# Attention fused with two MLPs on one core: row loads of the norms held behind key loads, queries loaded to 64 partitions

## The chip, the cores and the metric

One core of a Trainium2 chip. The time is device microseconds from launch to end of the whole fused kernel, median of several runs; one further execution was profiled. Engines: TensorE (PE, with its weight loads PEld), VectorE (DVE), ScalarE (ACT), GpSimd (POOL) and SyncE (SP, which here only issues DMAs).

## The reference

Attention over 4 x 12 heads, 448 rows, head size 64, then two MLPs over all 1792 tokens:

```python
def rmsnorm(x, g):
    rms = np.sqrt(np.mean(x * x, axis=-1, keepdims=True) + 1e-06)
    return x / rms * g
q_n, k_n = (rmsnorm(q, g_q), rmsnorm(k, g_k))
scores = scale * np.matmul(q_n, k_n.transpose(0, 1, 3, 2))
attn = softmax(scores)
x = np.matmul(attn, v)              # to (1792, 768)
x = ((x @ w1) * (x @ w2)) @ w3 @ w_out
h = x @ w_in
out = (h * np.clip(h + 3.0, 0.0, 6.0) / 6.0) @ w_out2
```

## The kernel before, in words

A "unit" i is a pair of heads; there are 24. A "row" t is one step of the loop at the end of `attention`: unit t // 8, score tile t % 8. In each row the loop traces one score product (two matmuls, high and low part of the keys, L536 and L537), its scaling with the norms and row maximum on DVE (L543), an exponential on ACT (L555), the transposes and value product of a unit 8 rows back, then `fill`, and then the tasks that `at(t, ...)` has put on this row. `fill` adds the other work: the product W' = w3 w_out in the first third (`wprime`), later the first MLP (`layer1`, `layer2`), with the conversion of 64-bit weights (`convert`, L135 to L141, three DVE operations a piece). All loads go through one in-order SP queue (`dma`, L88).

The order written is only a priority: a scheduler simulates the program and places every instruction of an engine as early as its operands and its buffers allow; on the chip each engine then runs its list in order. `tc.issue_after(x)` adds one constraint: what is issued inside it stands behind x on x's engine.

The norms of a unit pair g need the rows of q and k with the 64 numbers of a row along the free axis. `load_nat` (L409) fetches them (tile nat, 112 x 1024, 448 KB, two buffers). `ssq` squares on ACT (L436), `ssum` reduces on DVE (L442), `rms1` (L448 to L451) and `rms2` (L460 to L466) take the inverse root for the pair, `small1` transposes it on PE (L477) and `small2` copies it, writes it to DRAM (rkd) and reads it back spread over partitions (rb), which the unit's first L543 needs. Task rows for an even unit i: square of unit i+2 at row 8i, reduction at 8i+2, `load_nat(i+4)` at 8i+3 and `load_nat(i+5)` at 8i+4, `rms1` at 8i+6, `rms2` at 8i+6, `small1` at 8i+8.

Keys and queries come a second time, head dimension on partitions: `load_k` (tile kr, one buffer, row 8i+5 for unit i+2) and `load_q` (tile qr, one buffer, row 8i+3 for unit i+2). Both DRAM arrays hold the 64 rows twice, one copy over the other. `qhi` writes Q = round(q g) on all 128 partitions (ACT, L505), `qlo` puts the rest q g - Q over partitions 64 to 127 (DVE, L510), so one product takes the high and the low part of the query. `ksplit` writes K in two parts (ACT L516, POOL L517).

`load_nat(i)` tries to hold itself behind the key load of unit i-2: `T.get(("kl", i - 2))`. A key load is known there only once `load_k` has been traced, and `load_k(i+2)` is traced at row 8i+5.

Of the kernel before, what the change touches and what calls it, by code (L numbers as in the profile page):

```python
# [12 lines left out]
F32 = mybir.dt.float32  # L13
# [3 lines left out]
AF = mybir.ActivationFunctionType  # L17
# [5 lines left out]
B, H, S, D = 4, 12, 448, 64  # L23
HP = H // 2
NP = B * HP
P = 128
# [20 lines left out]
def fused_kernel(ctx: ExitStack, tc: tile.TileContext, nat, qT, kT, vin, gq, gk,  # L47
                 w12, w3t, wo, win, wo2, outT):
    nc = tc.nc
# [15 lines left out]
    G = gs[:, 2:3]  # L65
# [21 lines left out]
    def dma(out, src):  # L87
        return nc.sync.dma_start(out, src)  # L88
# [7 lines left out]
    def at(t, fn, *a):  # L96
        tasks[max(t + SHIFT.get(getattr(fn, "__name__", ""), 0), now[0])].append((fn, a))
# [304 lines left out]
    T = {}  # L402
    anchors = {}

    def attention(ap, rate):
# [3 lines left out]
        def load_nat(i):  # L409
            if i < NP:  # L410
                T["nat", i] = ap.tile([CP, 4 * NC, D], F32, tag="nat", bufs=2, name="nat")
                a = T.get(("kl", i - 2))
                with ExitStack() as es:
                    if a is not None:
                        es.enter_context(tc.issue_after(a.ins))
                    dma(T["nat", i], nat[i].rearrange("p a b d -> p (a b) d"))

        def load_q(i):
            T["qr", i] = ap.tile([P, 2, S], F32, tag="qr", bufs=1, name="qr")
            dma(T["qr", i], qT[i])  # L420

        def load_k(i):
            T["kr", i] = ap.tile([P, 2, S], F32, tag="kr", bufs=1, name="kr")
# [78 lines left out]

        def qhi(i):
            T["Q", i] = q = ap.tile([P, 2, S], F32R, tag="Q", bufs=2, name="Q")
            nc.scalar.activation(q, T["qr", i], AF.Copy, scale=G)  # L505

        def qlo(i):
            a = slice(64, 128)
            q = T["Q", i]
            nc.vector.scalar_tensor_tensor(out=q[a], in0=T["qr", i][a], scalar=G[a, :], in1=q[a],  # L510
                                           op0=ALU.mult, op1=ALU.subtract)

        def ksplit(i):
# [133 lines left out]
        groups = {s: [s, s + 1] for s in range(0, NP, 2)}  # L647

        load_nat(0)
        load_nat(1)  # L650
        dma(gs[:, 0:1], gq)
        dma(gs[:, 1:2], gk)
        nc.vector.tensor_mul(G, gs[:, 0:1], gs[:, 1:2])
        load_q(0)
        load_k(0)
        open_wprime()
# [10 lines left out]
        first = ExitStack()  # L667
        first.enter_context(tc.issue_after(T["rbl"].ins))
        qhi(0)
        qlo(0)  # L670
        ksplit(0)
        for z in range(10):
            prep[0].step()
        load_q(1)
        load_k(1)
        for z in range(16):
            prep[0].step()
        load_nat(2)
        load_nat(3)

        for i in range(NP):
            t = 8 * i
            n = i + 1
            if n < NP:
                at(t, qhi, n)
                at(t + 1, qlo, n)
                at(t + 2, ksplit, n)
            at(t - 4, load_v, i)
            if i + 2 < NP:
                at(t + 3, load_q, i + 2)  # L690
                at(t + 5, load_k, i + 2)
            at(t + 1, vsplit, i)
            if i % 2 == 0 and i + 2 < NP:
                g = groups[i + 2]
                at(t, ssq, i + 2)
                at(t + 2, ssq, i + 3)
                at(t + 3, ssum, i + 2, g)
                at(t + 3, load_nat, i + 4)
                at(t + 4, ssum, i + 3, g)
                at(t + 4, load_nat, i + 5)  # L700
                at(t + 5, rms1, g)
                at(t + 6, rms2, g)
                at(t + 16, load_rb, i + 3)

            u = t + LG
            at(u + 2, rsum1, i)
            at(u + 6, xcopy, i, 0)
            at(u + 7, xadd, i, 0)
            at(u + 8, small1, i, None)
            at(u + 9, small2, i, None)  # L710
            at(u + 9, xcopy, i, 1)
            at(u + 10, xadd, i, 1)
            at(u + 13, xout, i)
            if i % 2 == 0 and i + 2 < NP:
                g = groups[i + 2]
                tasks[t + LG] = [z for z in tasks[t + LG] if z[0] is not small1]
                tasks[t + LG + 1] = [z for z in tasks[t + LG + 1] if z[0] is not small2]
                at(t + LG, small1, i - 1, g)
                at(t + LG + 1, small2, i - 1, g)

        t = -1
# [36 lines left out]
    with tc.tile_pool(name="att", bufs=2, side="left") as ap:  # L758
        attention(ap, rate)
# [45 lines left out]
    step, q = 0, 0  # L805
# [126 lines left out]
```

## Time and profile before

| | us |
|---|---|
| median of 3 runs | 1272.6 (1270.17 to 1278.13) |
| profiled execution, device time | 1276.18 |
| span of its profile, first to last instruction | 1274.3 |
| PE busy in the span | 1183.1 |
| DVE busy in the span | 795.1 |

A row of a stretch reads: its length, then for each engine the busy time and the number of instructions, the granted TensorE clock as a share of full speed (2.4 GHz), the mean busy share of the 16 DMA engines, and the GB/s that they moved. A row of a group of instructions reads: line, engine, operation, output and inputs, shapes, count, then busy us, mean ns of one, and the idle time of the engine just before them.

### The profile page before, as it was taken

The page shows a single profiled execution, that of the slowest core. Times are in us where ns is not written, and L with a number is a line of the kernel's source. Part 1 is how long each engine was busy: PE and PEld are TensorE (multiplying, and loading weights), DVE is VectorE, ACT ScalarE, POOL GpSimd, SP SyncE. Part 2 cuts the span into 40 slices and gives each one's busy share as a digit, 9 for nine tenths or more (in the row PEclk, how much of TensorE's full clock was granted, in tenths as well). Part 3 has the DMA queues.
Part 4 walks back from the last instruction along what each step waited for, and adds up shares of the span by engine and source line. Part 5 has one row for each costly group of instructions (what it writes and reads, how often), then busy time and mean ns, then how long its engine had stood idle before and what let it go on. Part 6 is the DMA issues. An engine that isn't in the chain of part 4 may idle for free.

```text
span 1274.3 us, 16884 instructions
## 1 busy us (share of the span) xinstructions
PE 1183.1 (93%) x5868; PEld 1033.9 (81%) x5868; DVE 795.1 (62%) x1524; ACT 678.8 (53%) x1305; POOL 463.6 (36%) x292
## 2 busy tenths in 40 slices
PE   3587998888889999999999999889999999999998
PEld 2355987667668999999998998778999999999997
DVE  6989789989993578768643446994433343343332
ACT  5887667866783566766642223444533353344332
POOL 4334324624443112222111003445454454545542
PEclk9698998989999999999999999899999999999999
DMA  7898664666688666676349983450100020001001
GB/s 248 253 256 243 202 193 167 194 229 228 211 274 306 209 217 199 235 225 220 134 163 382 348 323 113 158 173 25 60 28 1 1 87 1 1 1 44 1 1 44
DMA packets 64693, 203.72 MB, mean 160 GB/s; under 512 B 8544, under 2 KB 25440, under 8 KB 64608
## 3 DMA queue, kind: packets, MB, share of 16 engines
q1 hardware_dynamic: 64608, 202.65, 48.2%
q8 instruction: 46, 0.75, 0.2%
q14 instruction: 39, 0.32, 0.1%
HBM read 173.93 MB, written 28.68 MB: 159 GB/s over the span
## 4 chain that ended last, share of the span: by engine, by line
PE 67%; DMA 11%; DVE 10%; issue 5%; ACT 3%; POOL 2%; SPq 1%; DVEq 0%; POOLq 0%; ACTq 0%
PE bank L80 8%; PE bank L82 8%; PE bank L81 8%; PE acc L81 6%; PE acc L82 6%; PE acc L80 5%; PE h L80 5%; PE h L81 5%; PE h L82 5%; PE bank L562 3%; DMA raw<-in_w_dram 2%; DVE wf L141 2%; DMA wr<-in_wo_dram 2%; PE bank L536 2%; PE bank L537 2%
## 5 line engine op out<-in xcount | busy, mean ns | idle before, releaser
L800 POOL TENSOR_TENSOR wis<-wf,wis 128x768 fp32r<-128x768 f32 x63 | 119.8, 1902 | 234.1 <-ACT wis L799 234.1
L872 DVE SCALAR_TENSOR_TENSOR u<-u,h 128x448 f32<-128x448 f32 x64 | 39.5, 618 | 217.3 <-ACT u L871 217.3
L800 POOL TENSOR_TENSOR wos<-wf,wos 128x768 fp32r<-128x768 f32 x64 | 119.0, 1860 | 103.6 <-ACT wos L799 103.6
L80 PE MATMUL bank<-xhl,ws 128*128 128x448 f32 x384 | 145.1, 378 | 7.7 <-ACT ws L285 6.3
L543 DVE CUSTOM_DVE_ANT_0 PP<-bank,rb,rq 112x448 f32<-112x448 f32 x192 | 129.1, 677 | 31.9 <-PE bank L537 27.4
L82 PE MATMUL bank<-xhl,ws 128*128 128x448 f32 x384 | 143.9, 375 | 4.9 <-POOL ws L287 4.9
L81 PE MATMUL acc<-g,wos 128*128 128x448 f32 x384 | 144.3, 376 | 3.8 <-DVE g L876 3.7
L555 ACT ACTIVATE PP<-PP,mx 112x448 f32<-112x448 f32 x192 | 127.4, 664 | 37.4 <-DVE mx L550 34.2
L80 PE MATMUL acc<-g,wos 128*128 128x448 f32 x384 | 138.5, 371 | 5.5 <-ACT g L875 5.5
L82 PE MATMUL acc<-g,wos 128*128 128x448 f32 x384 | 143.2, 373 | 0.0
L81 PE MATMUL bank<-xhl,ws 128*128 128x448 f32 x384 | 142.5, 371 | 0.1
L80 PE MATMUL h<-x2h,wis 128*128 128x448 f32 x378 | 139.0, 368 | 0.0
L81 PE MATMUL h<-x2h,wis 128*128 128x448 f32 x378 | 138.9, 368 | 0.0
L82 PE MATMUL h<-x2h,wis 128*128 128x448 f32 x378 | 137.5, 364 | 0.4 <-POOL wis L800 0.4
L876 DVE TENSOR_TENSOR g<-u,g 128x448 fp32r<-128x448 f32 x64 | 97.9, 1529 | 33.6 <-ACT g L875 33.6
L871 ACT ACTIVATE u<-h,half 128x448 f32<-128x448 f32 x64 | 40.4, 631 | 143.2 <-PE h L82 143.2
L536 PE MATMUL bank<-K,Q 128*112 128x448 f32 x192 | 78.3, 409 | 37.5 <-DVE mx L543 25.0
L562 PE MATMUL bank<-ident,PP 112*128 112x112 f32 x672 | 97.0, 267 | 11.8 <-DVE xl L581 10.2
L562 PEld LDWEIGHTS bank<-ident,PP 112*128 112x128 f32 x672 | 80.5, 145 | 33.8 <-DVE xl L581 13.3
L571 ACT ACTIVATE xh<-bank 128x448 fp32r<-128x448 f32 (+1 forms) x156 | 83.0, 537 | 43.3 <-PE bank L562 38.4
L581 DVE TENSOR_TENSOR xl<-bank,xh 128x448 fp32r<-128x448 f32 x142 | 87.1, 615 | 25.5 <-ACT xh L571 23.8
L799 ACT ACTIVATE wos<-wf 128x768 fp32r<-128x768 f32 x64 | 54.1, 846 | 86.9 <-PE acc L82 86.7
(126 smaller groups left out, 2763.5 us busy)
## 6 DMA issues: line engine op xcount, KB each, us to landing
ws<-w12d SPq DMA_DIRECT2D x48, 768.0 KB, 5.1
ws<-wpd SPq DMA_DIRECT2D x32, 768.0 KB, 4.2
raw<-in_w_dram SPq DMA_DIRECT2D x32, 384.0 KB, 4.3
w12d<-ws SPq DMA_DIRECT2D x16, 768.0 KB, 6.0
wr<-in_win_dram SPq DMA_DIRECT2D x16, 768.0 KB, 4.5
wr<-in_wo_dram SPq DMA_DIRECT2D x16, 768.0 KB, 6.6
nat<-in_nat_dram SPq DMA_DIRECT2D x24, 448.0 KB, 5.9
qr<-in_qT_dram SPq DMA_DIRECT2D x24, 448.0 KB, 6.4
```

The lines of the kernel that those rows point to most:

```text
L80: nc.tensor.matmul(ps, lh, rh, start=first, stop=False)
L81: nc.tensor.matmul(ps, lh, rl, start=False, stop=False)
L82: return nc.tensor.matmul(ps, ll, rh, start=False, stop=last)
L536: nc.tensor.matmul(ps[:CP, :S], qs, k1[:, j, :], start=True, stop=False)
L543: anchors[8 * i + s].append(nc.vector.tensor_tensor_reduce(out=T["PP", i][:, c, sl], in0=ps[:CP, :S], in1=T["rb", i][:, sl], op0=ALU.mult, ...
L555: anchors[8 * i + s].append(nc.scalar.activation(v, v, AF.Exp, bias=T["m", i][:, 8 + s : 9 + s], accum_out=T["sum", i][:, s : s + 1]))
L562: nc.tensor.transpose(ps[:, c * CP : c * CP + CP], src[:, c, kb * P : kb * P + P], ident[:CP, :CP])
L571: nc.scalar.activation(hi, ps, AF.Copy)
L581: nc.vector.tensor_sub(lo, ps, hi)
L799: nc.scalar.activation(t[:, 0, :], wf[q], AF.Copy)
L800: nc.gpsimd.tensor_sub(t[:, 1, :], wf[q], t[:, 0, :])
L876: nc.vector.tensor_sub(g[:, 1, :], u, g[:, 0, :])
```

## The change

Three edits. `load_nat` moves three rows later, to 8i+6 and 8i+7, behind the row in which `load_k(i+2)` is traced, and falls back to the key load of unit i-3, so that both row loads of a pair stand behind `load_k(i+2)`. `load_q` fetches one copy of the queries to partitions 0 to 63 (224 KB in place of 448 KB). `qhi` writes the high part on 64 partitions, and `qlo` reads partitions 0 to 63 and writes 64 to 127.

```diff
         def load_nat(i):
             if i < NP:
                 T["nat", i] = ap.tile([CP, 4 * NC, D], F32, tag="nat", bufs=2, name="nat")
-                a = T.get(("kl", i - 2))
+                a = T.get(("kl", i - 2)) or T.get(("kl", i - 3))
...
         def load_q(i):
-            T["qr", i] = ap.tile([P, 2, S], F32, tag="qr", bufs=1, name="qr")
-            dma(T["qr", i], qT[i])
+            T["qr", i] = ap.tile([D, 2, S], F32, tag="qr", bufs=1, name="qr")
+            dma(T["qr", i], qT[i][:D])
...
-            nc.scalar.activation(q, T["qr", i], AF.Copy, scale=G)
+            nc.scalar.activation(q[:D], T["qr", i], AF.Copy, scale=G[:D, :])
 
         def qlo(i):
-            a = slice(64, 128)
             q = T["Q", i]
-            nc.vector.scalar_tensor_tensor(out=q[a], in0=T["qr", i][a], scalar=G[a, :], in1=q[a],
+            nc.vector.scalar_tensor_tensor(out=q[D:], in0=T["qr", i], scalar=G[:D, :], in1=q[:D],
                                            op0=ALU.mult, op1=ALU.subtract)
...
                 at(t + 3, ssum, i + 2, g)
-                at(t + 3, load_nat, i + 4)
+                at(t + 6, load_nat, i + 4)
                 at(t + 4, ssum, i + 3, g)
-                at(t + 4, load_nat, i + 5)
+                at(t + 7, load_nat, i + 5)
```

## Rows read from the trace of the kernel before

**Rows 1.** The page's first part: busy time of each engine over the span
```profile
PE 1183.1 (93%) x5868; PEld 1033.9 (81%) x5868; DVE 795.1 (62%) x1524; ACT 678.8 (53%) x1305; POOL 463.6 (36%) x292
```

**Rows 2.** Stretches of the attention: engines, clock, DMA share, GB/s
```profile
core 0: us, PE busy (x) PEld busy (x) DVE busy (x) ACT busy (x) POOL busy (x), PEclk, DMA share, GB/s
0.00:60.00 60.00, 26.25 (x78) 17.14 (x79) 49.19 (x108) 40.46 (x77) 23.32 (x20) 0.85 0.81 252
60.00:130.00 70.00, 56.65 (x243) 37.23 (x242) 64.93 (x152) 54.81 (x114) 27.44 (x21) 0.87 0.92 250
130.00:240.00 110.00, 101.85 (x550) 89.05 (x550) 94.03 (x238) 78.46 (x170) 38.54 (x27) 0.94 0.63 201
240.00:400.00 160.00, 138.76 (x687) 112.18 (x686) 141.85 (x338) 113.51 (x259) 76.25 (x57) 0.94 0.69 229
400.00:660.00 260.00, 260.00 (x1438) 235.81 (x1437) 169.39 (x412) 157.40 (x338) 54.82 (x39) 1.00 0.62 206
```

**Rows 3.** The chain of waits from 60 to 130 us, shares by line
```profile
by line: DMA raw<-in_w3t_dram 17.7%; DMA raw<-in_wo_dram 10.8%; DVE raw L136 7.8%; DMA rkd<-rks 7.6%; DMA rsd<-rss 6.6%; DMA rsb<-rsd 6.2%; DMA wpd<-wst 5.9%; DVE raw L138 5.5%; issue 5.5%; DVE raw L141 3.8%; DVE ss L442 3.6%; SPq L88 3.3%;
```

**Rows 4.** DMA issues by stretch: 0:60 (two), 60:130 (three), 130:240, 240:400
```profile
nat<-in_nat_dram SPq DMA_DIRECT2D x8, 448.0 KB, 9.3
kr<-in_kT_dram SPq DMA_DIRECT2D x5, 448.0 KB, 3.2
...
DMA packets 6593, 17.48 MB, mean 250 GB/s; under 512 B 865, under 2 KB 2273, under 8 KB 6586
nat<-in_nat_dram SPq DMA_DIRECT2D x12, 448.0 KB, 5.9
kr<-in_kT_dram SPq DMA_DIRECT2D x2, 448.0 KB
...
kr<-in_kT_dram SPq DMA_DIRECT2D x4, 448.0 KB, 3.3
...
kr<-in_kT_dram SPq DMA_DIRECT2D x6, 448.0 KB, 5.2
```

**Rows 5.** SP's queue in order of time: the key load of unit 6
```profile
121.68 0.33 SPq L88 DMA_DIRECT2D kr<-in_kT_dram  x1
```

**Rows 6.** DVE's groups from 60 to 130 us: the norms' reductions and arithmetic
```profile
L442 DVE TENSOR_REDUCE ss<-nat 112x16 f32<-112x1024 f32 x12 | 14.4, 1208 | 0.0
...
L461 DVE TENSOR_TENSOR rt<-rt,ss 112x32 f32<-112x32 f32 x5 | 1.8, 353 | 0.0
L462 DVE TENSOR_SCALAR rt<-rt 112x32 f32<-112x32 f32 x5 | 1.7, 348 | 0.0
L460 DVE TENSOR_TENSOR rt<-ry 112x32 f32<-112x32 f32 x5 | 1.7, 332 | 0.0
...
L464 DVE TENSOR_TENSOR rr<-ry,rt 112x32 f32<-112x32 f32 x3 | 1.1, 360 | 0.0
L448 DVE TENSOR_SCALAR ss<-ss 112x32 f32<-112x32 f32 x6 | 1.0, 169 | 0.0
```

**Rows 7.** DVE's groups from 240 to 400 us: the norms
```profile
L442 DVE TENSOR_REDUCE ss<-nat 112x16 f32<-112x1024 f32 x2 | 2.3, 1210 | 0.0
...
L460 DVE TENSOR_TENSOR rt<-ry 112x32 f32<-112x32 f32 x3 | 1.1, 373 | 0.0
```

**Rows 8.** The query's low part (min/median/max ns), then 128 partitions against 64
```profile
L510 DVE SCALAR_TENSOR_TENSOR Q<-qr,gs,Q x24: 1150/1635/3026, 10.1 to 595.6; 64x896 fp32r<-64x896 f32 x24
...
L581 DVE TENSOR_TENSOR xl<-bank,xh 128x448 fp32r<-128x448 f32 x58 | 35.7, 617 | 18.7 <-ACT xh L571 17.3
...
L583 DVE TENSOR_TENSOR xh<-bank,xh 64x448 fp32r<-64x448 f32 x10 | 6.2, 618 | 27.3 <-ACT xl L574 27.3
```

**Rows 9.** Stretches with loads to 128 partitions, then to 64 (columns as rows 2)
```profile
159.80:162.30 2.50, 2.50 (x17) 2.29 (x16) 2.47 (x10) 1.31 (x3) 0.00 (x0) 1.00 0.87 267
...
560.30:563.20 2.90, 2.90 (x18) 2.64 (x17) 2.09 (x5) 1.38 (x4) 0.00 (x0) 1.00 0.49 108
```

**Rows 10.** PE's waits from 0 to 60 us: who, total us, times, longest
```profile
PE bank L477 <- DVE rr L464: 2.3, 1, 2.3
```

## The prediction

> **What bounds the kernel now.** I read the page's first part, then stretches, then the chain, then the queues. Over the whole span PE is busy 93% [rows 1], but this is a mean over unlike stages. The stretches [rows 2] show two regimes: from 400 to 660 us PE has no idle time (260.00 of 260) and DVE has 91 us to spare; before 400 us PE is idle for 33.8, 13.4, 8.2 and 21.2 us, 76.5 in all, while DVE is busy 82% to 93%. So only what shortens the time up to 400 us counts, and what can be put off beyond it is free. The tightest stretch is 60 to 130 us: DVE 64.93 of 70, DMA share 0.92, both the highest of all, and a granted TensorE clock of 0.87, that is part of the time at 1.2 GHz, after the first stretch with its idle PE. The chain there [rows 3] is almost without PE: 28.5% are weight loads (raw), 26.3% the small transfers rkd, rsd, rsb and wpd, then the weights' conversion on DVE.
>
> In this stretch 12 of the 24 row loads of the norms are issued, after 8 before it, but only 7 key loads in both together [rows 4]. The row loads run up to ten units ahead of the units that need them. The code says why: at row 8i+3 the key load of unit i+2 isn't traced yet (row 8i+5), so the hold finds nothing and the scheduler places a row load as soon as a buffer is free. The DVE groups [rows 6] show the price: 14.4 us of reductions and 1.8 + 1.7 + 1.7 + 1.1 + 1.0 = 7.3 us of arithmetic, 21.7 of the 64.93.
>
> **The change, part by part.**
>
> *The hold.* Behind the change both row loads of a pair (i+4, i+5) stand behind the key load of unit i+2. From the counts of key loads [rows 4] I take what becomes due where. Up to 60 us five are issued (units 0 to 4), so pairs up to (6,7) are let go, as now; 60 to 130 us adds units 5 and 6, the latter only at 121.68 [rows 5], so pair (8,9) arrives at its end; 130 to 240 adds 7 to 10, 240 to 400 adds 11 to 16. One pair costs DVE two reductions of 1.21 us and about 7.3 / 5 = 1.5 us of arithmetic [rows 6], 3.9 us.
>
> From 60 to 130 us one pair, (6,7), is left of the norms: 21.7 - 3.9 = 17.8 us less DVE. The DMA loses ten row loads of 0.459 MB and two halves of a query load of 0.229 MB: 5.05 of 17.48 MB [rows 4]; at a share of 0.92 of 70 us for 17.48 MB, 3.7 us a MB, that is 18.6 us. Both limits thus give way by the same amount. PE comes next: it has 13.4 us of idle time in the stretch [rows 2]. I let the stretch shrink by these 13.4 us. The other ends: 17.8 if the clock also recovers (56.65 us x 0.87 = 49.3 at full clock, which fits into 52), and nothing if the waits for small transfers in the chain [rows 3] are a matter of their own latency.
>
> From 130 to 240 us two pairs are processed today and two after the change: no difference. From 240 to 400 us one pair's reductions (2.3 us) and three groups' arithmetic (3 x 1.5) are there today [rows 7], 6.8 us; after it three pairs, 11.7: 4.9 us more DVE. DVE is idle 18.2 us in this stretch [rows 2], so between 0 and 4.9 is paid; no row is nearer to one end, so I take the middle, 2.4. The six row loads that come into it, 2.75 MB, cost 160 x 0.69 / 36.6 (229 GB/s x 160 us) = 3.0 us a MB, 8 us of DMA time where 50 are idle, and six halved query loads take 1.4 MB back: nothing. Three pairs, (18,19) to (22,23), move beyond 400 us: 3 x 3.9 = 12 us DVE, hidden under its 91 idle there. The squares on ACT move with them and are covered, ACT being the less busy engine everywhere [rows 2].
>
> The SP queue: behind a key load that waits for its buffer now also stand two row loads. Behind these are weight loads; but today a row load waits for its own buffer in the same queue, so I count no difference, with the waits of PE named below as the risk.
>
> *The queries.* ACT and DVE still go through 896 columns. For DVE a 64-partition form takes as long as a 128-partition one, 618 against 617 ns, and the 64-partition row is one that writes partitions 64 to 127 from 0 to 63 as `qlo` will [rows 8]; `qlo`, 1150 ns at best and 1635 at the median, stays. I count 0 for ACT and DVE. The transfer is halved. Its price isn't in the trace, so by the nearest rows [rows 9]: with loads to 128 partitions the engines move 267 / 0.87 = 307 GB/s of busy time, in the stretch with the two 64-partition loads 108 / 0.49 = 220. A full query load is 0.459 / 307 = 1.49 us, a half one between 0.75 and 1.04 us. I take 1.04, a saving of 0.45 us. It tells only where the DMA presses and I have not counted it yet, from 0 to 60 us: five loads, 2.2 us, of which I put 1 us on the path (0 to 2.2).
>
> The Trainium skill (SBUF — State Buffer, section "Door 1: The DMA port swizzle") speaks against this part: 64 partitions from 0 reach only half of the ports, so half the bytes would go at half the rate. The rows lie between that rule and an unchanged rate (220 against 307, not 153). By the rule the 1 us would be 0 and the sum 11.0 in place of 12.0.
>
> *The sum.* -13.4 + 2.4 - 1.0 = -12.0 us. The profiled execution took 1276.2 us (a span of 1274.3 and 1.9 around it), which gives 1264.2; it lay 3.6 us above the median of the runs, so against that I predict 1272.6 - 12.0 = 1260.6 us. What is won before 400 us stays won, since afterwards PE goes through a fixed list without a gap.
>
> **Rivals.** About 1%, 12.7 us, is what a measurement of this kernel can tell from no change.
>
> *More than that.* Both resources keep their shares in the freed stretch, the clock recovers, the 4.9 us are covered: -17.8 - 2.2 = -20.0, 1252.6 us. For it: DVE and DMA give way alike. Against it: PE would need the full clock at once, and the chain holds latencies.
>
> *Hidden anyway.* The stretch is set by the latencies in its chain, rkd, rsd, rsb and wpd with 26.3%, and by weight loads whose place in the order stays [rows 3]. Then the relief is nothing, the late cost 2.4 and the queries -1: 1274 us. Against it: the raw loads, 28.5%, wait in a DMA queue of which 29% of the bytes go.
>
> *Slower: PE waits for the norms.* Today the scaled roots of a pair are ready long before the transpose (L477) that stands in PE's list two rows behind `rms2`; the one time this failed, in the first stretch, PE waited 2.3 us [rows 10]. With the rows held back, the chain load, square, reduction, root, transpose follows the key load by the length of DVE's and ACT's queues. It decides once the last multiply of a pair comes on DVE later than PE reaches its transpose. Eleven pairs at 2.3 us cost 25.3: 1260.6 + 25.3 = 1285.9. Against it: the load is let go at row 8i+5 and the transpose stands at row 8i+24, 19 rows later; from 60 to 130 us, the tightest stretch, two key loads and so two units of 8 rows are issued in 70 us, 4.4 us a row, so some 80 us of room.
>
> *The change doesn't do what it says.* If the hold changed nothing in the order, only the queries' 1 us would be left: 1271.6. As the key load of unit i+2 is traced one row ahead of the new place, I hold that for unlikely.
>
> **How the numbers follow.** The forecast, 7 to 17 us won: 0.45, about half of it on either side of 12.7. More: 0.20. Hidden: 0.20. Slower by waits: 0.12. No hold: 0.03. Faster by over 1%: 0.20 + 0.23 = 0.43; within: 0.22 + 0.20 + 0.03 = 0.45; slower: 0.12. The likeliest case's own range is 1255.6 to 1265.6. The range reaches from 1242, twice the sum's relief and more than the second case (the scheduler lays out the whole program anew), to 1282, short of the slower case.
>
> **What would show it.** Right: between two key loads two row loads, and the last pair's after the key load of unit 20 rather than by 230 us; in the stretch after 60 us fewer than four reductions, its DMA share clearly under 0.92; the last conversions of the first MLP's weights some 12 us earlier; `qlo` still at 1150 ns at best. Wrong: the units 2 to 4 at the same times as today in spite of fewer reductions (hidden), idle time of PE before L477 in many pairs (the slower case), or row loads as far ahead as today (no hold).

## The result and the profile after

The changed kernel takes 1288.6 us (median of 4, 1287.23 to 1291.69) against 1273.8 us of the kernel before beside it (median of 4, 1270.17 to 1278.13): a ratio of 1.0132, interval 1.0094 to 1.017. It is 1.3% slower, where 1260.6 us was forecast, and outside the range. The profiled execution took 1287.23 us with a span of 1285.5, 11.2 us more than the span before. (In the lines after, code below L506 stands one line higher than before: L542 for L543, L509 for L510, L561 for L562.)

The first view is the table of stretches, columns as in [rows 2]:

```profile
0.00:60.00 60.00, 27.68 (x69) 16.04 (x70) 46.62 (x102) 37.19 (x70) 22.96 (x20) 0.87 0.73 222
60.00:130.00 70.00, 66.26 (x327) 50.58 (x326) 58.17 (x144) 50.79 (x112) 30.05 (x22) 0.91 0.66 210
130.00:240.00 110.00, 93.73 (x498) 80.20 (x497) 97.72 (x240) 80.20 (x176) 42.10 (x29) 0.92 0.60 180
240.00:400.00 160.00, 133.64 (x626) 105.31 (x625) 139.87 (x329) 110.23 (x246) 69.23 (x51) 0.88 0.69 214
400.00:660.00 260.00, 258.17 (x1413) 232.72 (x1412) 171.19 (x427) 158.45 (x343) 51.42 (x37) 1.00 0.66 213
```

Read PE's count of matmuls, which is progress, against [rows 2]. From 60 to 130 us the forecast relief is there: 327 for 243, PE idle 3.7 us for 13.4, DMA share 0.66 for 0.92. From 130 to 240 us 52 matmuls are lost again (498 for 550), from 240 to 400 another 61 (626 for 687), 57 of them of the filler, which waits for the converted weights (274 for 331). In that last stretch PE is idle 26.4 us for 21.2, and its clock is granted at 0.88 for 0.94: one matmul takes 133.64 / 626 = 213 ns for 202. Over 626 matmuls that is 7.2 us, beside 5.1 us of idle time. The whole kernel shows the same: PE runs 5868 matmuls in both profiles, with 6.7 us more busy time after (1189.8 for 1183.1) and 4.5 us more idle time, so more than half of the loss is matmuls that took longer. DVE, of which the prediction feared more work from 240 to 400 us, is busy 139.87 us for 141.85: its total did not grow.

Where the order of loads changed shows in SP's queue in order of time, 270 to 372 us, row and weight loads of the first MLP (`raw<-in_w_dram`) alone:

```profile
274.71 1.29 SPq L88 DMA_DIRECT2D nat<-in_nat_dram  x2
279.37 3.46 SPq L88 DMA_DIRECT2D raw<-in_w_dram  x2
...
301.71 0.33 SPq L88 DMA_DIRECT2D raw<-in_w_dram  x1
...
333.79 0.89 SPq L88 DMA_DIRECT2D nat<-in_nat_dram  x2
336.66 0.35 SPq L88 DMA_DIRECT2D raw<-in_w_dram  x1
```

The hold does what it says: the row loads come in pairs behind every second key load, the first of each pair at 129, 176, 222, 275, 334, 388, 471 and 517 us; before, the last one was issued by 227 us. Three pairs thus come into the time in which the weights of the first MLP are loaded, converted and split, where there was none. The chain of waits from 280 to 372 us (start, us, what) says what that does; after:

```profile
by line: DMA raw<-in_w_dram 26.6%; issue 15.9%; POOL ws L287 6.9%; ACT PP L554 4.5%; DVE PP L542 4.0%; DVE raw L136 3.4%; PE bank L80 3.2%; PE bank L82 2.8%; PE bank L81 2.7%; ACT raw L135 2.6%; DVE raw L141 2.6%; PE bank L561 2.5%; ACT xh 
...
279.37 8.93 DMA raw<-in_w_dram
...
300.38 1.31 POOL ws L287
301.71 4.75 DMA raw<-in_w_dram
...
335.60 1.04 POOL ws L287
336.66 6.52 DMA raw<-in_w_dram
343.63 0.63 DVE raw L136
344.25 1.12 DVE ss L442
345.44 0.47 DVE raw L141
...
352.46 1.90 DVE ss L448
354.36 1.85 POOL ws L287
```

and before, the same stretch:

```profile
289.20 1.04 POOL ws L287
290.25 4.87 DMA raw<-in_w_dram
...
298.57 1.00 POOL ws L287
299.58 4.91 DMA raw<-in_w_dram
304.51 3.52 DMA raw<-in_w_dram
```

In both, most `raw` loads start just when a split on POOL (L287) ends: of the 25 that need a freed buffer, 22 before and 16 after start within 0.1 us of the end of the split that frees theirs. That is a loop of three buffers (L269): a piece is loaded, converted by ACT and DVE, split by ACT and POOL, and only then is its buffer free for the next load. What lengthens one turn of it delays the pieces behind. In these chains the piece of a load behind two row loads is 8.93 and 6.52 us long, that of the others 3.5 to 4.9. At 344.25 and 352.46 the norms' reduction and first root operation stand in the chain themselves, the latter with 1.90 us for what takes 0.17 at best (the last section says what held it). The share of the weight loads in the chain is no larger after (26.6% for 27.6%), and few of their landings were recorded: from 240 to 400 us five before, 3.4 to 6.2 us, and three after, 6.5, 6.6 and 8.9 us, of which only the last is behind row loads.

From the issue of the fifth of these loads to the last split this loop ran from 233.4 to 386.8 us before (153.4 us) and from 228.5 to 397.2 us after (168.7). It begins 4.9 us earlier and ends 10.4 us later; the whole kernel ends 11.2 us later. The parts of a turn, as means over its 28 pieces, show where the time went: from a load's issue to the first conversion 6.1 us for 5.1, the conversion 6.9 for 6.7, from there to the split's end 3.7 for 3.9, and from that to the issue of the load into the freed buffer 0.6 for 0.2. So nearly all of it lies in front of the first conversion, and little of it inside the conversion.

The third difference is at the start, DVE in order of time (start, us, line, operation; in brackets the idle time and its end). Before:

```profile
8.64 0.18 DVE L448 TENSOR_SCALAR ss<-ss 112x32 f32<-112x32 f32 x1
10.12 1.15 DVE L510 SCALAR_TENSOR_TENSOR Q<-qr,gs,Q 64x896 fp32r<-64x896 f32 x1 [1.30 <-ACT Q L505]
...
21.16 0.68 DVE L543 CUSTOM_DVE_ANT_0 PP<-bank,rb,rq 112x448 f32<-112x448 f32 x1 [0.59 <-DMA rb<-rkd]
```

After:

```profile
9.38 1.15 DVE L509 SCALAR_TENSOR_TENSOR Q<-qr,gs,Q 64x896 fp32r<-64x896 f32 x1 [0.95 <-ACT Q L505]
10.55 1.96 DVE L448 TENSOR_SCALAR ss<-ss 112x32 f32<-112x32 f32 x1
...
26.38 0.68 DVE L542 CUSTOM_DVE_ANT_0 PP<-bank,rb,rq 112x448 f32<-112x448 f32 x1 [5.31 <-DMA rb<-rkd]
```

With the first query halved, its split is placed ahead of the root of the first norms, that root starts 1.9 us later and runs 1.8 us longer, and the first score comes at 26.4 us for 21.2.

### The profile page after: what moved, and what is told of

It reads as the page before. It is cut to its first block, busy times and chain, and to the rows that moved or that the text cites. A ratio compares the mean times of both kernels' runs of the same rounds, so it can differ in the third digit from the quotient of the medians.

```text
span 1285.5 us, 16863 instructions
## 1 busy us (share of the span) xinstructions
PE 1189.8 (93%) x5868; PEld 1037.5 (81%) x5868; DVE 793.6 (62%) x1524; ACT 677.9 (53%) x1305; POOL 464.8 (36%) x292
## 2 busy tenths in 40 slices
DMA packets 63157, 198.21 MB, mean 154 GB/s; under 512 B 8544, under 2 KB 25440, under 8 KB 63072
## 4 chain that ended last, share of the span: by engine, by line
PE 61%; DMA 13%; DVE 13%; issue 5%; ACT 4%; POOL 2%; SPq 1%; ACTq 0%; DVEq 0%; POOLq 0%
PE bank L80 7%; PE bank L81 7%; PE bank L82 7%; PE acc L81 5%; PE acc L82 5%; PE acc L80 5%; PE h L80 5%; PE h L81 5%; PE h L82 5%; PE bank L561 3%; DMA raw<-in_w_dram 3%; DMA wr<-in_wo_dram 2%; DMA wr<-in_win_dram 2%; DVE PP L542 2%; DMA wpd<-wst 2%
## 5 line engine op out<-in xcount | busy, mean ns | idle before, releaser
L542 DVE CUSTOM_DVE_ANT_0 PP<-bank,rb,rq 112x448 f32<-112x448 f32 x192 | 128.5, 676 | 41.3 <-PE bank L536 32.9
L80 PE MATMUL bank<-xhl,ws 128*128 128x448 f32 x384 | 146.7, 383 | 5.1 <-ACT ws L285 3.7
L82 PE MATMUL bank<-xhl,ws 128*128 128x448 f32 x384 | 144.7, 377 | 5.4 <-POOL ws L287 5.3
L80 PE MATMUL acc<-g,wos 128*128 128x448 f32 x384 | 138.9, 372 | 5.2 <-ACT g L874 5.1
L82 PE MATMUL acc<-g,wos 128*128 128x448 f32 x384 | 143.2, 373 | 0.0
L80 PE MATMUL h<-x2h,wis 128*128 128x448 f32 x378 | 139.1, 368 | 0.0
L82 PE MATMUL h<-x2h,wis 128*128 128x448 f32 x378 | 137.4, 363 | 0.4 <-POOL wis L799 0.4
L561 PE MATMUL bank<-ident,PP 112*128 112x112 f32 x672 | 98.1, 269 | 19.2 <-DVE xl L580 17.0
L561 PEld LDWEIGHTS bank<-ident,PP 112*128 112x128 f32 x672 | 80.7, 145 | 42.1 <-DVE xl L580 16.4
```

The source lines that it names most:

```text
L80: nc.tensor.matmul(ps, lh, rh, start=first, stop=False)
L82: return nc.tensor.matmul(ps, ll, rh, start=False, stop=last)
L542: anchors[8 * i + s].append(nc.vector.tensor_tensor_reduce(out=T["PP", i][:, c, sl], in0=ps[:CP, :S], in1=T["rb", i][:, sl], op0=ALU.mult, ...
L561: nc.tensor.transpose(ps[:, c * CP : c * CP + CP], src[:, c, kb * P : kb * P + P], ident[:CP, :CP])
```

## The experiments

Fifteen kernels ran, in four lots, each lot beside the kernel before. The last three columns are read from each trace: the start of the 151st matmul of the filler (L80 to L82, W' and the first MLP), which tells how far the relief of the early stretch got, when the loop begins and ends, and how many row loads are issued inside it.

| kernel | ratio (95%) | 151st filler matmul | loop of first MLP's weights | row loads in it |
|---|---|---|---|---|
| before | 1 | 138.0 | 233.4 to 386.8 = 153.4 | 0 |
| the change | 1.0132 (1.0094 to 1.0170) | 120.6 | 228.5 to 397.2 = 168.7 | 6 |
| e1 queries only | 1.0066 (1.0044 to 1.0087) | 143.8 | 235.7 to 389.3 = 153.6 | 0 |
| e2 hold only | 1.0005 (0.9987 to 1.0023) | 123.4 | 226.2 to 386.7 = 160.5 | 6 |
| e3 hold, early pairs | 1.0035 (1.0015 to 1.0054) | 123.6 | 235.4 to 389.0 = 153.6 | 2 |
| e4 hold, late pairs | 1.0067 (1.0041 to 1.0093) | 127.5 | 219.7 to 398.4 = 178.7 | 6 |
| e5 first query as before | 0.9884 (0.9846 to 0.9922) | 114.3 | 213.8 to 362.5 = 148.7 | 4 |
| e6 before, four buffers | 0.9935 (0.9915 to 0.9956) | 141.5 | 234.5 to 368.4 = 133.9 | 0 |
| e7 hold, four buffers | 0.9943 (0.9921 to 0.9966) | 121.4 | 221.0 to 357.9 = 136.9 | 4 |
| e8 hold, late norms left out | 0.9923 (0.9900 to 0.9946) | 123.6 | 223.9 to 379.2 = 155.3 | 0 |
| e9 roots ahead of query | 1.0081 (1.0063 to 1.0100) | 117.8 | 225.6 to 403.9 = 178.3 | 6 |
| e10 queries from unit 1 | 1.0069 (1.0040 to 1.0098) | 143.4 | 232.7 to 393.1 = 160.4 | 0 |
| e11 hold, queries from unit 2 | 1.0018 (1.0001 to 1.0034) | 114.9 | 219.4 to 390.1 = 170.7 | 6 |
| e12 hold, queries from unit 12 | 1.0059 (1.0036 to 1.0083) | 119.5 | 221.9 to 386.5 = 164.6 | 4 |
| e13 change, four buffers | 0.9986 (0.9970 to 1.0002) | 120.9 | 228.1 to 368.8 = 140.7 | 4 |
| e14 e5, four buffers | 0.9920 (0.9897 to 0.9944) | 116.6 | 219.7 to 366.0 = 146.3 | 4 |
| e15 change, late norms left out | 0.9910 (0.9880 to 0.9940) | 120.1 | 223.9 to 370.1 = 146.2 | 0 |

**Parts of the change alone.** e1 has the query edits, e2 the hold. e3 and e4 hold only the row loads of the units named:

```diff
# e3, against before (load_nat of units below 12)
+                a = T.get(("kl", i - 2)) or (T.get(("kl", i - 3)) if i < 12 else None)
+                at(t + (6 if i < 8 else 3), load_nat, i + 4)
+                at(t + (7 if i < 8 else 4), load_nat, i + 5)
# e4 (units from 12 on)
+                a = T.get(("kl", i - 2)) or (T.get(("kl", i - 3)) if i >= 12 else None)
+                at(t + (6 if i >= 8 else 3), load_nat, i + 4)
+                at(t + (7 if i >= 8 else 4), load_nat, i + 5)
```

> The kernel before with the three query edits alone; row loads as before. Theory A (the loss is made by row loads that now come while the first MLP's weights are loaded, 240 to 400 us): not slower than before by more than the late start, so 0 to +5 us, 1273 to 1279, and no loss of matmul progress between 290 and 365 us. Theory C (the query edits make the loss: the smaller load lands first and pushes the first pair's roots back): first score row on DVE at 26 us in place of 21, and most of the 15 us, 1283 or more. Theory B (the new layout of the lists as a whole): anything within 10 us either way.

> The kernel before with the hold alone (later rows, fallback to the key load of unit i-3); queries as before. A: slower than before by 6 to 13 us, 1280 to 1287; ahead of before by 10 us or more at 135 us, behind it by 365 us, the weight loads that follow two row loads landing after 7 to 9 us in place of 4 to 5. C: about 1262, the early gain kept. B: no forecast.

> The hold for pairs (4,5) to (10,11) alone; later pairs placed as before (rows 3 and 4, nothing held), which lets them all load between 175 and 235 us, ahead of the first MLP's weights; queries as before. A: the early gain is kept, 8 to 14 us faster than before, 1260 to 1266. B: as unclear as any other layout, within 8 us of before. C: 1262 as with the hold alone.

> The hold for pairs (12,13) to (22,23) alone; pairs up to (10,11) placed as before; queries as before. A: no early gain and the late loss, 8 to 16 us slower than before, 1282 to 1290, with the loss between 240 and 400 us. B: within 8 us of before. C: no slower than before.

Measured: 1281.45, 1274.6, 1278.91 and 1282.17 us, against 1273.9 before. Neither part is a gain; the hold alone is worth nothing, the queries alone cost 0.66%. e4 shows half of the change's loss with the queries left as they were: three pairs inside the loop, and the loop at 178.7 us. Theory A had its time right, but not the missing early gain: in e4, too, only 12 row loads come before 130 us in place of 20, and the 151st matmul is 10.5 us early. Otherwise A failed, in e1 (7.6 us slower), in e2 (0.7 us) and in e3, and so did theory C in e1 and e2, although e1 had the late first score (26.2 us). e3 was to keep the early gain without the late cost and did not. Its late row loads, free again, were all issued between 188 and 242 us, and its lead of 14.4 us at the 151st matmul was gone when the loop began (235.4). In e3, that is, the loads and norms taken out of the early stretch were paid for ahead of the loop, so the loop alone does not account for every loss.

**The loop of three buffers.** e6 is the kernel before and e7 the hold alone, each with a fourth buffer (room for it from another tile); e8 is the hold alone without the norms of the pairs from (12,13) on:

```diff
# e6, e7, and e13, e14 below
-                raw[u].append(fetch(pool, w12[u // 2, 1 - u % 2][:, h * NH : h * NH + NH], NH, "raw", 3))
+                raw[u].append(fetch(pool, w12[u // 2, 1 - u % 2][:, h * NH : h * NH + NH], NH, "raw", 4))
...
-        for _ in range(3):
+        for _ in range(4):
             load()
...
-                T["xs", i] = ap.tile([P, S], F32, tag="xs", bufs=8, name="xs")
+                T["xs", i] = ap.tile([P, S], F32, tag="xs", bufs=6, name="xs")
# e8, and e15 below; ssq, ssum, rms1 and rms2 return alike, rms2 with the roots of pair (10,11)
-            if i < NP:
+            if i < min(NP, 12):
```

e5 is the changed kernel with the first unit's query loaded and split as before, to test the start:

```diff
+            h = P if i < 1 else D
+            T["qr", i] = ap.tile([h, 2, S], F32, tag="qr", bufs=1, name="qr")
+            dma(T["qr", i], qT[i][:h])
...
# qhi and qlo alike
```

> The changed kernel with the first unit's query load and split as before (128 partitions); units 1 to 23 keep the query edits, the hold stays. Theory S (the queries cost by the start alone: unit 0's smaller load lands first, its split goes ahead of the first pair's roots, and the first score comes 5 us late): first score row on DVE at 21 us again and 1275 to 1280, near the hold alone. Theory Q (the later query edits cost as well, by the order that they bring): still 1284 or more.

> The kernel before with four in place of three buffers for the raw weights of the first MLP (the room comes from tile xs, six buffers in place of eight). Theory W (from 240 to 385 us the three-buffer loop of these weights, load, conversion, split, next load, sets the end): the pieces follow each other in under 4.8 us in place of 5.0 and the time falls by 4 to 15 us, 1259 to 1270. Theory V (DVE's total work sets it): no change, within 4 us.

> The hold alone (queries as before) with four buffers for the raw weights, as in the run before this one. W: the early gain is no longer given back, so faster than the same without the hold by 5 to 12 us, 1252 to 1264. V: within 4 us of before.

> The hold alone, and for pairs (12,13) to (22,23) row loads, squares, reductions and roots are left out (the roots of pair (10,11) stand in; the output is then another one). W: without row loads between 240 and 400 us the weights' loop is back at 5.0 us a piece or less and the early gain is kept: 6 to 12 us faster than before, 1262 to 1268, at most. If the late norms cost nothing at all (theory B, the layout): 1274 as with the hold alone. V: 20 us less DVE work of which two thirds before 400 us, 1258 to 1262.

Measured, against 1273.2 us: e5 1259.9, e6 1265.16, e7 1264.95, e8 1263.6. Theory W's forecast held in e6 and e8, and e7 lies 1 us above it; e8 alone does not tell W from V, whose ranges touch there. For e5 both forecasts failed. One buffer more shortens the loop by 19.5 us in the kernel before and by 23.6 with the hold, with DVE's work nearly unchanged (793.2 for 795.1 us, 796.5 for 795.2); about 8 us of either reach the kernel's time. Tile xs has two buffers fewer in these kernels, which no run tried alone. e6's row from 240 to 400 us in the table of stretches:

```profile
240.00:400.00 160.00, 143.41 (x712) 119.83 (x711) 128.94 (x308) 106.65 (x242) 73.42 (x55) 0.94 0.74 246
```

Beside the last but one of [rows 2]: 25 more matmuls at the same clock, and DVE with 12.9 us less to do. The conversions of the stretch are the same (84 operations for 83), but the filler runs 387 matmuls for 331, and there are 38 scalings of scores on DVE for 46: the filler got ahead of the attention. So the loop, not DVE's total, limits the filler here. e5 was a surprise in its size, 28.7 us under the changed kernel, where its first score comes 5.5 us earlier.

**Is it the start?** e9 is the changed kernel with the first query's split put behind that first root; e10 has no hold and halves the queries from unit 1 on; e11 and e12 are the changed kernel with the queries halved from unit 2 and 12 on:

```diff
# e9, against the changed kernel
-        qlo(0)
+        with tc.issue_after(T["r1"].ins):
+            qlo(0)
# e10: i < 1, e11: i < 2, e12: i < 12
+            h = P if i < 1 else D
```

> The changed kernel, all query loads halved, and unit 0's low query part issued on DVE behind the first operation of the first pair's roots (L448), as it stood in the kernel before. Theory S (the late start is what unit 0's edit costs): first score row at 21 us and 1255 to 1266, as when unit 0 keeps the full load. Theory L (every edit lays the lists of all engines out anew, and the layouts differ by some 15 us either way, whatever the edit does): first score row at 21 us all the same, but any time from 1258 to 1290.

> No hold; the query edits for units 1 to 23 alone. S: the late start is gone, so 4 to 9 us faster than with all query edits, 1272 to 1277 (or as fast as 1262 if the halved loads themselves win). L: anywhere from 1260 to 1290.

> The hold, and the query edits for units 2 to 23; unit 1 differs from the run with units 1 to 23, a difference of one load of 0.229 MB and no more. S and any theory of DMA relief: within 3 us of that run, 1257 to 1263. L: may differ by 5 us or more either way.

> The hold, and the query edits for units 12 to 23, whose loads are issued after 240 us. DMA relief in the first 130 us (what was predicted): none is left, so as the hold alone, 1272 to 1277. L: anything from 1258 to 1290.

Measured, against 1271.88 us: 1283.58, 1281.89, 1274.5 and 1281.37. In e9 the root stands ahead of the split again, at 9.07 us, and the first score comes at 23.0, 3.4 us earlier than in the changed kernel, and yet it is 0.81% slower than before. In e10 to e12 the first score is at 20.9 to 22.2 us, and all three are slower than before. Theory S failed in e9 to e11, so the late start is at most a part of the loss, and in e12 the forecast from DMA relief failed. Theory L's times held, but its ranges, some 30 us wide, could hardly fail. e5 and e11 differ in the load of one single unit, 0.229 MB, and in 14.6 us. Most of that difference arises in the loop (148.7 and 170.7 us), and no part of the edit lies there: what differs is the order that the scheduler has written for all engines. With four row loads in it, e5's loop is shorter than that of the kernel before, so row loads in the loop do not lengthen it in every order.

**The changed kernel with the loop relieved.** e13 is the changed kernel with four buffers, e14 is e5 with four, e15 the changed kernel without the norms of the pairs from (12,13) on.

> The changed kernel (hold and all query edits) with four buffers for the raw weights of the first MLP, room from tile xs. Theory W (the changed kernel reaches 240 us ahead and loses it in the three-buffer loop of these weights): the loop from its fifth load to its last split takes 145 us or less in place of 169 and the time is 1258 to 1270, near the same step on the kernel before (1265) and on the hold alone (1265), whatever the layout. Theory L alone (a bad layout of all lists, no one place): still 1277 or more.

> The changed kernel with unit 0's query as before, and four buffers for the raw weights. W: this kernel's loop with three buffers already took 149 us, so little is left to win: 1250 to 1262. L: anywhere from 1255 to 1275.

> The changed kernel; for pairs (12,13) to (22,23) row loads, squares, reductions and roots are left out (the roots of pair (10,11) stand in; another output). W with the row loads as what lengthens the loop: the loop takes 150 to 158 us in place of 169 and the time is 1268 to 1278. If the late norms are innocent (L): 160 us or more and 1282 or more.

Measured, against 1273.29 us: 1271.43, 1261.94 and 1261.09. The fourth buffer takes the changed kernel from 1.0132 to 0.9986, and the loop from 168.7 to 140.7 us (W's forecast of the loop held, its time lay 1.4 us too low). It gives e5 nothing (0.9884 and 0.9920): its loop was short already. Without the late norms the ratio falls to 0.9910, 2.2 points. e15's row from 240 to 400 us:

```profile
240.00:400.00 160.00, 144.19 (x738) 116.81 (x739) 132.63 (x320) 111.69 (x249) 68.97 (x52) 0.99 0.75 248
```

738 matmuls for the 626 of the changed kernel, at a clock of 0.99 for 0.88. The late start is the same in e15 (26.4 us), so the start alone does not make the loss. What was left out are six row loads, their squares and reductions in the loop, with the ones behind it. Without them the four parts of a turn are 4.9, 6.5, 3.4 and 0.3 us. The gain is larger than the whole loss and than W had forecast, e8 gained 0.8 points by the same cut, and the order changed as well: that this work makes most of the loss is supported, not isolated. A count over the three-buffer kernels supports it too. The five with six row loads in the loop take 160.5 to 178.7 us for it, 171.4 on the mean, the five with none 146.2 to 160.4, 153.8 on the mean; but a loop that is long for another reason also takes in a later pair.

Whether the transfers or the operations cost it wasn't tried alone. For the transfers speaks a second count. In each of the eleven kernels with row loads in the loop, the `raw` loads issued within 6 us behind one had to wait longer from issue to first conversion than the rest, on the mean: 7.2 us against 6.0 in the changed kernel (3 loads of 28), 8.4 against 5.9 in e2 (6), 8.7 against 5.8 in e4 (9), 8.2 against 4.9 in e5 (7). In the changed kernel this explains little, as only three loads are meant and the other 25 also wait longer than the 5.1 us of the kernel before; why these do stays open.

**The kernels together.** Seven kernels have the full hold or the late one with three buffers (the change, e2, e4, e5, e9, e11, e12), three have none (before, e1, e10). On the mean the loop begins at 222.2 us in the seven and at 233.9 in the three, 11.7 us earlier; it lasts 167.2 us against 155.8; and it ends at 389.3 against 389.7. On the mean the early gain is given back in the loop; that the ends agree to 0.4 us is luck, since the seven ends lie between 362.5 and 403.9 us. In the ratios it is the same: 1.0035 and 1.0045 on the mean. About this mean the seven scatter from 0.988 to 1.013, and the changed kernel is the slowest of them. What follows the loop takes 887.5 us before and 888.3 after, so this pair was decided by the loop's end; with four buffers it takes 898 to 903 us, and a part of their shorter loops does not arrive.

e5 was the fastest kernel of all with the whole computation, 1.2% under the kernel before, but its neighbours say that this is one happy order among several. The fourth buffer is the sounder gain: it shortened the loop in the three kernels in which it was long, and gave 0.65% on the kernel before.

## Why the prediction was wrong

**What bounds the kernel: half right.** That the time up to 400 us counts held for the change: the loop ended 10.4 us later, the kernel 11.2. But of the pairs that are put off, only those that go beyond 400 us were free; those that stop on the way, in the loop, were not, and the prediction priced them at 2.4 us.

**60 to 130 us, -13.4 us: right.** One pair's reductions are left in it, as forecast; PE's idle time fell by 9.6 us, and one matmul took 203 ns for 233, 10 us over 327, at a clock of 0.91 for 0.87, which alone would give 223. The 151st filler matmul came 17.4 us earlier, between the forecast and the rival "more". In every kernel with any hold it came at 114 to 128 us, without one at 138 to 144.

**130 to 240 us, "no difference": wrong.** I counted two pairs on either side. There are three, and PE was idle 16.3 us for 8.2:

```profile
L442 DVE TENSOR_REDUCE ss<-nat 112x16 f32<-112x1024 f32 x6 | 7.3, 1210 | 3.6 <-ACT nat L436 3.6
```

The third pair is (12,13), let go at 222 us and reduced at 229. Of the 17.4 us only 4.9 were left at the loop's beginning, so 12.5 us were lost here, nearly as much as in the loop. That the matmuls which had come forward used up the stock of converted weights sooner is argued, not shown. The chain of waits from 130 to 228 us has another candidate: the stores of W' (`wpd<-wst`) make up 20.9% of it after and do not stand in it before. What the 12.5 us went to stays open.

**240 to 400 us, +2.4 us: the step that failed.** The amount came out near, 10.7 us of norms on DVE for the 11.7 forecast, partly by luck, since four reductions came for six and the arithmetic took 5.9 us for 4.5:

```profile
L442 DVE TENSOR_REDUCE ss<-nat 112x16 f32<-112x1024 f32 x4 | 4.8, 1210 | 0.3 <-ACT nat L436 0.3
L448 DVE TENSOR_SCALAR ss<-ss 112x32 f32<-112x32 f32 x2 | 2.1, 1056 | 0.0
```

The price was wrong, 15.3 us of loop for the 2.4. I priced the work by DVE's idle time in the stretch and the six loads, 8 us of DMA time "where 50 are idle", at nothing. Both are means over the stretch, and it runs by a loop whose turn is the sum of a landing, the place in two engines' queues, and a split. What comes in front of one of these steps can lengthen the turn, however idle the engine is afterwards; here a turn grew from 15.9 to 17.2 us, 1.0 us of it between a load's issue and the first conversion. The prediction shows the chain of waits only from 60 to 130 us [rows 3]; from 280 to 372 us it shows this loop before the change: weight loads make up 27.6% of it, most of them begun at the end of a split.

**The queries, -1.0 us: wrong in sign.** They cost 0.66% alone. ACT and DVE took as long as forecast: `qlo` at least 1144 ns for 1150. The halved load saved bytes (198.21 MB for 203.72 in all); that it saved time the profiles do not show: of 24 landings three each were recorded, 4.0, 7.0 and 12.7 us after, 5.3, 6.4 and 7.7 before. The Trainium skill (SBUF — State Buffer, section "Door 1: The DMA port swizzle") says that partitions 0 to 63 reach half of the ports; these six landings do not contradict it. The prediction's 220 GB/s for loads to 64 partitions was no price either: a load of 768 KB to 128 partitions (`ws<-w12d`) was issued inside that stretch [rows 9], at 561.57. And at the start an earlier query was not harmless: its split pushed the root of the first norms back. As e10 is 0.69% slower without the late start, and orders scatter by more than that, why the queries cost is not shown.

**The rivals.** "Hidden anyway", 1274 us, comes nearest to the held kernels' mean, but for another reason: the relief was real and was given back. (The lower end of the forecast's range, 1242, is called twice the sum's relief, but twice 12.0 us would give 1248.6; nothing hangs on it.) "Slower", 1285.9 us, has the right number with a mechanism that did not happen. After 60 us no wait of PE for L464 at L477 appears in either kernel; the one in the first stretch grew from 2.3 to 4.7 us, which belongs to the late start:

```profile
PE bank L477 <- DVE rr L464: 4.7, 1, 4.7
```

**What stays open.** The mechanism accounts, on the mean of seven kernels, for a gain that comes to nothing. The further 1.0% of this one kernel may be partly its start (e9 lies 0.5 points lower, but its loop is 9.6 us longer) and for the rest the order that the scheduler happened to write: similar edits lie up to 2.5% apart. Why one order makes a loop of 149 us and another one of 179 was not settled, nor what the 12.5 us ahead of the loop went to.

## What to carry to other kernels

Price work that is moved by the loop it lands in, not by the idle time of its engine: where a few buffers go round through load, conversion and split, what comes in front of one of these steps can be paid as a longer turn, and here a buffer more was worth more than the rearrangement. Follow the chain of waits in the stretch where the work arrives, not only in the one it leaves. And where a scheduler lays out the whole program anew, make several neighbouring variants before reading 1% as the effect of an edit.

## What the runs showed of the hardware

A very short DVE operation beside a POOL operation can take as long as POOL does. L448, 0.18 us before, took 1.96 us after, and it ended at 12.51, when this POOL operation (start 10.27) ended at 12.48:

```profile
10.27 2.21 POOL L516 TENSOR_TENSOR K<-kr,K 128x896 fp32r<-128x896 f32 x1 [8.96 <-ACT K L515]
```

The kernel before has the same, L460 with 1.98 us, from 11.31 to 13.29, beside POOL's L517 from 11.14 to 13.24. In its neighbourhood, with POOL idle, these operations take 0.18 us. It recurs in both traces: of the norms' short operations (L448 and L460 to L466) 14 before and 18 after took more than 0.4 us, and each of the 32 ended 0.03 to 0.05 us behind an operation of POOL. The norms' price on DVE thus depends on what POOL does: from 240 to 400 us L448 had a mean of 1.06 us after. The 1.90 us of L448 in the chain above are such a case; POOL was splitting keys until 354.36:

```profile
351.45 2.91 POOL L516 TENSOR_TENSOR K<-kr,K 128x896 fp32r<-128x896 f32 x1
```

The Trainium skill (SBUF — State Buffer, section "A bandwidth-pool intuition that's wrong (but worth ruling out)") says that GpSimd and some VectorE operations exclude each other altogether; the times here agree with it.

A load of the queries to 64 partitions also kept SP busy longer than one of double the size to 128: 477 ns at the median of 24 for 333.
